# An attention and expert kernel: a chunk's right operands formed over two units, with raw weights in tiles of their own and the next pair's attention in every unit

## The chip, the cores and the metric

One Trainium2 chip, one core. A core has engines with their own instruction queues, each working through its queue in order: TensorE (PE; its weight loads stand as PEld), VectorE (DVE), ScalarE (ACT), GpSimd (POOL), and SyncE (SP), which here issues nearly all DMA transfers. The metric is the device time of one execution in microseconds (us).

## The reference, cut to what matters

```python
# q, k, v: (8, 8, 576, 64); p: (8, 8, 32, 64); w1: (4, 512, 1024); w2: (4, 1024, 512)
def sm_attn(qq, kk, vv):
    s = scale * np.matmul(qq, kk.transpose(0, 1, 3, 2))
    a = np.exp(s - np.max(s, axis=-1, keepdims=True))
    a = a / (np.sum(a, axis=-1, keepdims=True) + 1e-09)
    return np.matmul(a, vv)
p_packed = sm_attn(p, k, v)            # 32 packed tokens attend to all 576
x = sm_attn(q, p_packed, p_packed)     # all tokens attend to the packed ones
# x becomes (8*576, 512); pr = domain_probs, each row divided by its sum
for e in range(4):
    h = np.maximum(x @ w1[e], 0.0)
    out += pr[:, e:e + 1] * (h @ w2[e])
```

## The kernel before, in words

The work is split into 64 **units**. A unit is one batch (576 tokens) times one **chunk**, which is half an expert (512 of its 1024 hidden columns), so there are 8 chunks. Batches go in **pairs**: the units of the first pair are chunk 0 with batch 0, chunk 0 with batch 1, chunk 1 with batch 0, and so on (L283), 16 units for each of four pairs. In a pair of units the unit of the lower batch is called even, that of the upper batch odd.

A unit has two stages. `mm1_group` (L293) makes a block of the hidden layer, 24 matmuls of 128x288 each, four times a unit; VectorE multiplies it with the probabilities into a tile `ablk` (L311). `product` (L376) makes one of seven products of Strassen's kind, 12 matmuls each; their left operands are `ablk` blocks or sums of them (`sblk`, L328), and the right ones are blocks of w2 or differences of them. Every operand is kept as two parts, a rounded high part, cast by ScalarE (`hi_of`, L101), and the remainder, made by a subtraction (`lo_of`, L107). For the left operands the result is the tile `st` (four buffers), with the remainder on GpSimd; for the right ones it is `tt` (eight buffers). VectorE adds a product to its accumulator (`acc`, L394), or ScalarE copies it there when the chunk is the first (L392). The left operand of product i+2 is made while product i runs, and the hidden blocks of the next unit are made between the products of this one (`GROUPS`, L531).

`t_form` (L346) makes the seven right operands of a chunk: two raw halves of w2's chunk are loaded (L353), in-place differences t1 to t4 are taken (L366), and for each operand there is a cast on ScalarE and a subtraction on GpSimd (L369, L370). This is done in the first pair alone: each `tt` is stored to DRAM (`t_store`), and the three later pairs load it back (`t_load`). In the first pair it is done for chunk c+1 in the odd unit of chunk c, a step after each product (L573); its raw halves go into the tiles `kt` and `vt` of the pool `att`, which the attention uses too for k, q and v.

The attention of the next pair of batches also runs beside the units, as generators that are moved a step after certain products (`back`, L571): `pack_unit` (L140) for the packed tokens, and `tok_unit` (L213) for all tokens, each twice, for two halves of the heads. `AT_FIRST` (L533) says in which step (2 x chunk + 1 if odd) of the first pair each starts. `g_form` (L259) multiplies the packed tokens with the next chunk's w1 (tile `wraw`) into `ghl`, the weights of `mm1_group`.

PSUM has four double tiles `dbl`, which all matmuls share. The order of an engine's instructions isn't that of the code alone: the tile framework's scheduler puts the instructions of all generators into one order for each engine when the program is built.

The first 43 us or so are a prologue: attention of the first two batches, right operands of chunk 0 and the hidden blocks of unit 0.

## Time and profile before

| | us |
|---|---|
| median of three runs | 1331.51 (1331.44 to 1331.95) |
| the profiled execution | 1326.61 |
| its span, first to last instruction | 1324.8 |
| TensorE busy in the span | 1260.2 (95%) |
| VectorE busy | 950.8 (72%) |
| GpSimd busy | 862.5 (65%) |
| ScalarE busy | 474.8 (36%) |

The program is one long stretch of matmuls on TensorE with the other engines beside it, so it is read by pairs of units. A mark that recurs once in each pair of units is the group of 32 matmuls on `wraw` in `g_form`; from one such mark to the next is a *step pair* below. In the first pair of batches the marks start at 54.64, 105.72, 152.57, 198.74, 241.07, 284.15, 326.26 and 368.20 us, and the first one of the second pair of batches is at 407.91. Step pairs of the first pair of batches are counted from 0 (54.64 to 105.72) to 7 (368.20 to 407.91); those of the second pair, from 407.91 to 721.73, likewise.

### The profile page before, as it was taken

To read this page: it belongs to the slowest core of one execution; us is meant where nothing else is said; L and a number is where in the kernel's file an instruction comes from. 1 tells how busy PE (TensorE), PEld (TensorE's weight loads), DVE (VectorE), ACT (ScalarE), POOL (GpSimd) and SP (SyncE) were. 2 spreads that over 40 slices of the span, in tenths; PEclk is the share of its full clock that TensorE was granted. 3 is DMA by queue.
4 is the path that set the end of the run, shared out by engine and by line. 5 is a ranking of instruction groups with operands and counts; after the bars stand their busy time and mean duration, and the time that the engine had idled before them with its cause. 6 is when DMAs were issued, how large, how long until landed. Compare 5 with 4: busy or idle time off the path is not lost.

```text
span 1324.8 us, 26645 instructions
## 1 busy us (share of the span) xinstructions
PE 1260.2 (95%) x10720; PEld 1179.9 (89%) x10720; DVE 950.8 (72%) x1334; ACT 474.8 (36%) x784; POOL 862.5 (65%) x578
## 2 busy tenths in 40 slices
PE   4798998999999999999999999999999999999997
PEld 2697888889999989999999998999999999999996
DVE  5766779688685665888677566698668566666668
ACT  4353433434325423333333433333232533333231
POOL 5675787879887454467569554566657755555656
PEclk8999999999999999999999999999999999999999
DMA  9526643452465455544346554344454443344422
GB/s 359 199 82 214 205 162 114 177 186 105 187 208 165 157 175 175 188 148 136 119 133 215 175 171 151 127 150 150 124 153 175 159 134 123 123 152 137 127 96 72
DMA packets 84634, 208.98 MB, mean 158 GB/s; under 512 B 8608, under 2 KB 27168, under 8 KB 84512
## 3 DMA queue, kind: packets, MB, share of 16 engines
q1 hardware_dynamic: 83840, 207.13, 46.5%
q8 instruction: 86, 1.41, 0.4%
q14 instruction: 36, 0.29, 0.1%
q10 hardware_dynamic: 672, 0.15, 0.1%
HBM read 168.37 MB, written 38.87 MB: 156 GB/s over the span
## 4 chain that ended last, share of the span: by engine, by line
PE 74%; POOL 11%; DVE 6%; issue 5%; DMA 3%; ACT 1%; DVEq 0%; POOLq 0%; ACTq 0%; SPq 0%
PE dbl L66 70%; POOL st L108 5%; PE dbl L74 4%; POOL tt L108 3%; DMA kt<-in_w 2%; DVE sblk L328 1%; POOL kt L366 1%; DVE ghl L108 1%; DVE ablk L311 1%; POOL xl L108 1%; DVE acc L444 1%; DVE acc L409 1%; PE dbl L69 1%; POOL acc L444 1%; DMA pnd<-pb 1%
## 5 line engine op out<-in xcount | busy, mean ns | idle before, releaser
L66 PE MATMUL dbl<-st,tt 128*128 128x288 f32 x5376 | 771.7, 297 | 20.6 <-DVE ghl L108 8.3
L66 PEld LDWEIGHTS dbl<-st,tt 128*128 128x128 f32 x5376 | 731.3, 188 | 56.2 <-issue 27.6
L108 POOL TENSOR_TENSOR st<-sblk,st 128x576 fp32r<-128x576 f32 x256 | 394.4, 1548 | 250.9 <-ACT st L103 248.0
L66 PE MATMUL dbl<-xh,ghl 128*128 128x288 f32 x2048 | 416.7, 295 | 0.0
L108 POOL TENSOR_TENSOR st<-ablk,st 128x576 fp32r<-128x576 f32 x192 | 290.7, 1516 | 160.4 <-ACT st L103 159.8
L394 DVE TENSOR_TENSOR acc<-dbl,acc 128x576 f32<-128x576 f32 x385 | 288.6, 752 | 116.3 <-PE dbl L66 115.6
L66 PEld LDWEIGHTS dbl<-xh,ghl 128*128 128x128 f32 x2048 | 330.2, 189 | 0.0
L66 PE MATMUL dbl<-xl,ghl 128*128 128x288 f32 x1024 | 304.2, 297 | 18.1 <-DVE ablk L311 8.4
L311 DVE SCALAR_TENSOR_TENSOR ablk<-dbl,pbt 128x576 f32<-128x576 f32 x256 | 192.5, 752 | 166.0 <-PE dbl L66 164.5
L103 ACT CAST st<-sblk 128x576 fp32r<-128x576 f32 x256 | 173.1, 677 | 328.5 <-DVE sblk L328 230.1
L103 ACT CAST st<-ablk 128x576 fp32r<-128x576 f32 x192 | 129.6, 675 | 264.5 <-PE dbl L66 254.8
L66 PEld LDWEIGHTS dbl<-xl,ghl 128*128 128x128 f32 x1024 | 193.1, 189 | 20.7 <-DVE ablk L311 10.0
L328 DVE TENSOR_TENSOR sblk<-ablk 128x576 f32<-128x576 f32 x128 | 122.4, 956 | 9.2
L103 ACT CAST ghl<-dbl 128x512 fp32r<-128x512 f32 x128 | 71.9, 587 | 96.9 <-PE dbl L74 42.3
L108 DVE TENSOR_TENSOR ghl<-dbl,ghl 128x512 fp32r<-128x512 f32 x128 | 85.0, 684 | 24.5 <-ACT ghl L103 22.8
L328 DVE TENSOR_TENSOR sblk<-ablk,sblk 128x576 f32<-128x576 f32 x64 | 63.2, 988 | 3.1
L74 PE MATMUL dbl<-wraw,ppbd 64*32 64x512 f32 x1024 | 64.2, 595 | 0.3 <-ACT acc L392 0.3
L108 POOL TENSOR_TENSOR tt<-kt,tt 128x512 fp32r<-128x512 f32 x35 | 50.5, 1444 | 13.3 <-ACT tt L103 13.3
L328 DVE TENSOR_TENSOR sblk<-sblk,ablk 128x576 f32<-128x576 f32 x64 | 57.3, 895 | 1.4
L444 POOL TENSOR_TENSOR acc<-acc,acc 128x576 f32<-128x576 f32 x28 | 47.5, 1707 | 10.2 <-DVE acc L394 10.2
L392 ACT COPY acc<-dbl 128x576 f32<-128x576 f32 x56 | 35.6, 642 | 43.1 <-PE dbl L66 42.8
L103 ACT CAST tt<-kt 128x512 fp32r<-128x512 f32 x35 | 21.6, 621 | 46.1 <-DVE kt L366 16.7
(60 smaller groups left out, 442.4 us busy)
## 6 DMA issues: line engine op xcount, KB each, us to landing
tt<-td SPq DMA_DIRECT2D x168, 512.0 KB, 4.0
wraw<-in_w SPq DMA_DIRECT2D x128, 256.0 KB, 3.8
td<-tt SPq DMA_DIRECT2D x56, 512.0 KB, 4.4
kt<-in_k SPq DMA_DIRECT2D x16, 576.0 KB, 5.1
kt<-in_q SPq DMA_DIRECT2D x16, 576.0 KB, 5.3
pbt<-pnd SPq DMA_DIRECT2D x32, 288.0 KB, 4.0
out<-acc SPq DMA_DIRECT2D x32, 288.0 KB, 2.3
vt<-in_v SPq DMA_DIRECT2D x16, 512.0 KB, 5.8
```

The costliest lines, as they stand in the source:

```text
L66: on_pe(nc.tensor.matmul(**kw))
L69: on_pe(nc.tensor.transpose(**kw))
L74: ins = nc.tensor.matmul(**kw).ins
L103: nc.scalar.copy(out=dst, in_=src)
L108: eng.tensor_tensor(out=dst, in0=src, in1=hi.bitcast(F32), op=ALU.subtract)
L311: nc.vector.scalar_tensor_tensor(out=a, in0=ps[:, :, 0:HS], scalar=0.0, in1=pbt[b][:, ts].rearrange("p (o t) -> p o t", o=1).broadcast_to( ...
L328: nc.vector.tensor_tensor(out=t, in0=blk(x), in1=blk(y), op=op)
L366: eng[m].tensor_tensor(out=blk[place], in0=blk[x], in1=blk[y], op=ALU.subtract)
L392: nc.scalar.copy(out=accs[b, i], in_=psv)
L394: nc.vector.tensor_tensor(out=accs[b, i], in0=psv, in1=accs[b, i], op=ALU.add)
L409: nc.vector.tensor_tensor(out=dst, in0=x, in1=y, op=op)
L444: eng.tensor_tensor(out=m[dst], in0=m[x], in1=m[y], op=op)
```

## The change

Four edits, all in what the first pair of batches does.

1. Right operands of chunk c+1 are formed over both units of chunk c: three of them in the even one, after products 1, 3 and 5, and four in the odd one, after products 1 to 4 (`FORM`). `tt` has ten buffers in place of eight. A smaller scratch for dynamic DMA (`dynamic_dma_scratch_size=1024`) belongs to it; the kernel has no such DMA.
2. The raw halves of w2 have tiles of their own, `rw0` and `rw1`, one buffer each, and are loaded in the odd unit before, after products 3 and 5; those of chunk 1 before the first unit.
3. The subtraction t4 and the remainders of the operands `s3` and `a22` move from GpSimd to VectorE, beside t2 and t3, which were there. GpSimd keeps t1 and five remainders of seven.
4. The next pair's attention advances after every second product of every unit (before: in the even units alone, with all that was left drained at a unit's end for chunks 0 to 2), and its parts start at steps 3, 6, 9 and 12 in place of 2, 4, 6 and 10.

```diff
--- before.py
+++ after.py
@@ -336,38 +336,43 @@
     tt = {}
 
     def t_load(ch, i):
-        t = wpool.tile([P, 2, 2, DH], F32R, name="tt", bufs=8)
+        t = wpool.tile([P, 2, 2, DH], F32R, name="tt", bufs=10)
         nc.sync.dma_start(out=t.rearrange("p h f d -> p (h f d)").bitcast(F32), in_=td[ch][i])
         tt[ch, i] = t
 
     def t_store(ch, i):
         nc.sync.dma_start(out=td[ch][i], in_=tt[ch, i].rearrange("p h f d -> p (h f d)").bitcast(F32))
 
-    def t_form(ch, new, eng):
-
+    w2r = {}
+
+    def w2_load(ch, kh, new):
         e, hf = divmod(ch, F // FC)
-        raw = []
-        for kh in range(2):
-            r0 = hf * FC + kh * 2 * P
-            r = new([P, 2, DM], ("kt", "vt")[kh])
-            nc.sync.dma_start(out=r, in_=w2[e, r0:r0 + 2 * P, :].rearrange("(f p) d -> p f d", p=P))
-            raw.append(r)
+        r0 = hf * FC + kh * 2 * P
+        r = new([P, 2, DM], f"rw{kh}")
+        nc.sync.dma_start(out=r, in_=w2[e, r0:r0 + 2 * P, :].rearrange("(f p) d -> p f d", p=P))
+        w2r[ch, kh] = r
+
+    def raw_tile(shape, name):
+        return wpool.tile(shape, F32, name=name)
+
+    def t_form(ch, eng):
+
+        raw = [w2r.pop((ch, kh)) for kh in range(2)]
         blk = {
             "b11": raw[0][:, :, 0:DH], "b12": raw[0][:, :, DH:DM],
             "b21": raw[1][:, :, 0:DH], "b22": raw[1][:, :, DH:DM],
         }
-        yield
         of = {"a11": "b11", "a12": "b21", "s4": "b22", "a22": "t4", "s1": "t1", "s2": "t2", "s3": "t3"}
         how = {"t1": ("b12", "b11", "b11"), "t2": ("b22", "t1", "t1"), "t3": ("b22", "b12", "b12"), "t4": ("t2", "b21", "t2")}
         for i, name in enumerate(ORDER):
             n = of[name]
             for m in {"t3": ("t1", "t3"), "t2": ("t2",), "t4": ("t4",)}.get(n, ()):
                 x, y, place = how[m]
-                eng[m].tensor_tensor(out=blk[place], in0=blk[x], in1=blk[y], op=ALU.subtract)
+                eng.get(m, nc.gpsimd).tensor_tensor(out=blk[place], in0=blk[x], in1=blk[y], op=ALU.subtract)
                 blk[m] = blk[place]
-            t = wpool.tile([P, 2, 2, DH], F32R, name="tt", bufs=8)
+            t = wpool.tile([P, 2, 2, DH], F32R, name="tt", bufs=10)
             hi_of(t[:, 0], blk[n], nc.scalar)
-            lo_of(t[:, 1], blk[n], t[:, 0], nc.gpsimd)
+            lo_of(t[:, 1], blk[n], t[:, 0], eng.get(name, nc.gpsimd))
             tt[ch, i] = t
             yield
 
@@ -470,9 +475,6 @@
     def att_tile(b, shape, name):
         return att.tile(shape, F32, name=name, bufs=2 if name in ("kt", "a1") else 1)
 
-    def raw_tile(shape, name):
-        return att_tile(0, shape, name)
-
     hpool = ctx.enter_context(tc.tile_pool(name="hpool", bufs=1, reuse_waits="tile"))
     with ExitStack() as first:
         pools = [first.enter_context(tc.tile_pool(name=f"unit{u}", bufs=1)) for u in range(3)]
@@ -492,11 +494,12 @@
             tok_unit([b], g, unit_tile(2 * b + g), nc.gpsimd if g else nc.vector, nc.gpsimd if b else nc.scalar)
             for b in range(2) for g in range(NG)
         ]
-        forms = t_form(0, form_tile, {n: nc.gpsimd for n in ("t1", "t2", "t3", "t4")})
         norm_probs()
         for i in (0, 1, 0, 1):
             next(packs[i])
-        next(forms)
+        for kh in range(2):
+            w2_load(0, kh, form_tile)
+        forms = t_form(0, {})
         raws = w1_load(0)
         drain(wavefront(packs[:2], 1))
         for i in range(2):
@@ -530,7 +533,12 @@
     nothing = iter(())
     GROUPS = {1: ((0, 0),), 3: ((0, 1),), 4: ((1, 1),), 6: ((1, 0),)}
     GROUPS_FIRST = {4: ((0, 0), (0, 1)), 5: ((1, 1),), 6: ((1, 0),)}
-    AT_FIRST = ((2, pack_unit, 0), (4, pack_unit, 1), (6, tok_unit, 0), (10, tok_unit, 1))
+    AT_FIRST = ((3, pack_unit, 0), (6, pack_unit, 1), (9, tok_unit, 0), (12, tok_unit, 1))
+    FORM = ({1: 1, 3: 1, 5: 1}, {1: 1, 2: 1, 3: 1, 4: 1})
+    form_eng = {"t2": nc.vector, "t3": nc.vector, "t4": nc.vector, "s3": nc.vector, "a22": nc.vector}
+    for kh in range(2):
+        w2_load(1, kh, raw_tile)
+    tsteps = nothing
     AT_LATER = ((1, pack_unit, 0), (4, pack_unit, 1), (7, tok_unit, 0), (9, tok_unit, 1))
     sums, back = nothing, nothing
     for u, (sb, ch, b) in enumerate(units):
@@ -550,10 +558,8 @@
         if not odd and nsb < SB:
             gsteps = g_form([2 * nsb, 2 * nsb + 1], nch, raws)
         forming = odd and sb == 0 and ch + 1 < NCH
-        tsteps = nothing
-        if forming:
-            tsteps = t_form(ch + 1, raw_tile, {"t1": nc.gpsimd, "t2": nc.vector, "t3": nc.vector, "t4": nc.gpsimd})
-        next(tsteps, None)
+        if not odd and sb == 0 and ch + 1 < NCH:
+            tsteps = t_form(ch + 1, form_eng)
         for i in range(NPROD):
             product(u, i)
             n = i + LA
@@ -568,16 +574,17 @@
                 next(gsteps, None)
             if i == 4 and u + 2 < len(units) and units[u + 2][1] % 2 == 0:
                 load_probs(units[u + 2][2], units[u + 2][1] // 2)
-            if sb > 0 and i % 2 == 0 or sb == 0 and not odd and (i % 2 == 0 or ch < 3):
+            if i % 2 == 0:
                 next(back, None)
-            next(tsteps, None)
+            if i in FORM[odd]:
+                next(tsteps, None)
+            if forming and ch + 2 < NCH and i in (3, 5):
+                w2_load(ch + 2, i // 4, raw_tile)
             next(sums, None)
             if sb == 0 and not odd:
                 t_store(ch, i)
             if odd and nxt and not forming:
                 t_load(nxt[1], i)
-        if sb == 0 and ch < 3:
-            drain(back)
         drain(gsteps)
         drain(sums)
         if ch == NCH - 1 and b < B - 1:
@@ -610,7 +617,7 @@
         "w1": np.ascontiguousarray(moe_w1),
         "w2": np.ascontiguousarray(moe_w2),
     }
-    nc = bacc.Bacc("TRN2", target_bir_lowering=False, num_devices=1)
+    nc = bacc.Bacc("TRN2", target_bir_lowering=False, num_devices=1, dynamic_dma_scratch_size=1024)
     args = [
         nc.dram_tensor(f"in_{n}", arrays[n].shape, mybir.dt.from_np(arrays[n].dtype), kind="ExternalInput").ap()
         for n in _INS
```

What this does to the order on the engines, at three places. On ScalarE, around the casts of `ghl` in an even unit. Before (`kt` is the raw half of w2, `st` a left operand):

```order
L103 CAST st<-ablk 128x576 [waits PE_49,Pool_49]
L171 ACTIVATE a_1813,sm<-dbl,nb 128x576 [waits DVE_49,PE_49]
L103 CAST st<-ablk 128x576 [waits PE_49,Pool_49]
L171 ACTIVATE a_1822,sm<-dbl,nb 128x576 [waits DVE_49]
L103 CAST tt<-kt 128x512 [waits DMAHW3_49,DMAHW0_49]
L103 CAST ghl<-dbl 128x512 [waits PE_49]
L103 CAST ghl<-dbl 128x512 [waits DVE_49]
L103 CAST ghl<-dbl 128x512 [waits PE_49]
```

And now (`rw_1514` is a raw half of chunk 3, `at` an attention tile):

```order
L103 CAST tt<-rw_1514 128x512 [waits DMAHW2_49,DVE_49]
L103 CAST tt<-rw_1514 128x512 [waits DMAHW4_49,Pool_49]
L188 COPY at<-dbl 128x512 [waits PE_49]
L189 COPY at<-dbl 64x128
L103 CAST st<-ablk 128x576 [waits PE_49,Activation_49]
L103 CAST st<-sblk 128x576 [waits DVE_49,PE_49,Activation_49]
L103 CAST st<-ablk 128x576 [waits PE_49,Pool_49]
L103 CAST st<-ablk 128x576 [waits DVE_49,PE_49,Pool_49]
L103 CAST ghl<-dbl 128x512 [waits PE_49]
L103 CAST ghl<-dbl 128x512 [waits DVE_49]
L103 CAST ghl<-dbl 128x512 [waits PE_49]
L103 CAST st<-sblk 128x576 [waits PE_49,Pool_49]
```

Before, the first cast of a chunk, which waits for the raw half to land, stood right ahead of the casts of `ghl`; now the first three casts of a chunk stand ahead of a run of left operands, and the `ghl` casts have no raw half ahead of them in their unit.

On GpSimd, in an odd unit. Before (`kt` and `vt` raw halves, L366 the subtraction t4):

```order
L108 TENSOR_TENSOR tt<-kt,tt 128x512 [waits DMAHW5_49,Activation_49]
L108 TENSOR_TENSOR tt<-kt,tt 128x512 [waits DMAHW2_49,Activation_49]
L108 TENSOR_TENSOR st<-sblk,st 128x576 [waits Activation_49]
L108 TENSOR_TENSOR st<-ablk,st 128x576 [waits Activation_49]
L108 TENSOR_TENSOR tt<-kt,tt 128x512 [waits DMAHW3_49,Activation_49]
L108 TENSOR_TENSOR st<-ablk,st 128x576 [waits Activation_49]
L366 TENSOR_TENSOR kt<-kt,vt 128x2x256 [waits DMAHW6_49,Pool_49]
L108 TENSOR_TENSOR st<-sblk,st 128x576 [waits Activation_49]
L108 TENSOR_TENSOR tt<-kt,tt 128x512 [waits Activation_49]
L108 TENSOR_TENSOR tt<-vt,tt 128x512 [waits Activation_49]
L108 TENSOR_TENSOR tt<-vt,tt 128x512 [waits DMAHW7_49,Activation_49]
L108 TENSOR_TENSOR st<-sblk,st 128x576 [waits Activation_49] x2
```

And now, from the remainder of `s2` (the fourth operand) of chunk 4 to that of the third operand of chunk 5 (`rw_2075` and `rw_2129` are chunk 4's raw halves, `rw_2604` is chunk 5's, L371 is t1):

```order
L108 TENSOR_TENSOR tt<-rw_2075,tt 128x512 [waits DMAHW4_49,Activation_49]
L108 TENSOR_TENSOR st<-ablk,st 128x576 [waits Activation_49]
L108 TENSOR_TENSOR st<-sblk,st 128x576 [waits Activation_49]
L108 TENSOR_TENSOR tt<-rw_2129,tt 128x512 [waits DMAHW5_49,DMAHW0_49,Activation_49]
L108 TENSOR_TENSOR st<-ablk,st 128x576 [waits Activation_49]
L108 TENSOR_TENSOR tt<-rw_2129,tt 128x512 [waits DMAHW1_49,Activation_49]
L108 TENSOR_TENSOR st<-ablk,st 128x576 [waits Activation_49]
L108 TENSOR_TENSOR tt<-rw_2604,tt 128x512 [waits DMAHW7_49,DMAHW3_49,Activation_49]
L108 TENSOR_TENSOR st<-sblk,st 128x576 [waits Activation_49]
L371 TENSOR_TENSOR rw_2604<-rw_2604 128x2x256 [waits Pool_49]
L108 TENSOR_TENSOR st<-sblk,st 128x576 [waits Activation_49] x2
L108 TENSOR_TENSOR tt<-rw_2604,tt 128x512 [waits DMAHW6_49,Activation_49]
```

Before, seven instructions of the forming stand among these thirteen; now five remainders and t1 stand among seven left operands, and after the last row seven left operands follow with no forming between them. The first remainder of a chunk, which needs its raw half, stands four left operands behind the remainder of `s2`, ahead of where the code has it.

On VectorE, where t3 stands (it takes the second raw half, and waits for GpSimd's t1). Now, at the end of an odd unit (`acc` accumulators, `ablk` a hidden block out of PSUM):

```order
L311 SCALAR_TENSOR_TENSOR ablk<-dbl,pbt 128x576 [waits PE_49]
L328 TENSOR_TENSOR sblk<-ablk 128x576 [waits DVE_49]
L399 TENSOR_TENSOR acc_1101<-dbl,acc_1101 128x576 [waits PE_49]
L328 TENSOR_TENSOR sblk<-sblk,ablk 128x576 [waits DVE_49,Pool_49]
L399 TENSOR_TENSOR acc_1121<-dbl,acc_1121 128x576 [waits PE_49]
L371 TENSOR_TENSOR rw_2075<-rw_2129,rw_2075 128x2x256 [waits DMAHW5_49,DMAHW2_49,Pool_49]
L311 SCALAR_TENSOR_TENSOR ablk<-dbl,pbt 128x576 [waits PE_49]
L328 TENSOR_TENSOR sblk<-ablk,sblk 128x576 [waits DVE_49,Activation_49]
L108 TENSOR_TENSOR tt<-rw_2075,tt 128x512 [waits DMAHW1_49,Activation_49]
```

Before, in the even unit that holds the mark of step pair 4:

```order
L108 TENSOR_TENSOR ghl<-dbl,ghl 128x512 [waits Activation_49] x3
L394 TENSOR_TENSOR acc_796<-dbl,acc_796 128x576 [waits PE_49]
L366 TENSOR_TENSOR kt<-vt,kt 128x2x256 [waits DMAHW6_49,DMAHW7_49,DMAHW4_49,Pool_49]
L311 SCALAR_TENSOR_TENSOR ablk<-dbl,pbt 128x576 [waits PE_49]
L328 TENSOR_TENSOR sblk<-ablk 128x576 [waits DVE_49]
L394 TENSOR_TENSOR acc_845<-dbl,acc_845 128x576 [waits PE_49]
```

At both places a block that leaves PSUM stands right behind t3; what moved is t3 against the units, from behind the `ghl` remainders to behind the odd unit's last accumulation, and a remainder (the last row of the first piece) is new on this engine.

## Rows read from the trace of the kernel before

**Rows 1.** The page, part 1: busy us, share of the span and instructions of each engine.

```profile
PE 1260.2 (95%) x10720; PEld 1179.9 (89%) x10720; DVE 950.8 (72%) x1334; ACT 474.8 (36%) x784; POOL 862.5 (65%) x578
```

**Rows 2.** Windows: length, busy us (instructions) of each engine, granted clock, DMA share, GB/s.

```profile
54.64:105.72 51.08, 44.62 (x352) 41.46 (x352) 31.43 (x39) 23.02 (x41) 42.26 (x31) 0.93 0.34 119
105.72:368.20 262.48, 240.18 (x2058) 223.84 (x2057) 202.85 (x275) 100.54 (x172) 209.75 (x142) 0.99 0.48 169
...
407.91:448.08 40.17, 40.17 (x376) 37.44 (x375) 22.10 (x35) 19.00 (x34) 24.23 (x18) 1.00 0.53 176
448.08:683.02 234.94, 232.81 (x2011) 219.35 (x2010) 173.69 (x258) 79.04 (x126) 132.67 (x89) 1.00 0.47 153
...
241.07:284.15 43.08, 40.32 (x329) 37.72 (x329) 30.76 (x42) 14.72 (x24) 39.12 (x28) 0.96 0.58 210
...
569.28:608.21 38.93, 38.75 (x329) 36.18 (x329) 34.92 (x53) 14.22 (x22) 25.30 (x17) 1.00 0.48 160
```

**Rows 3.** Waits of TensorE from 105.72 to 368.20: total us, times, longest.

```profile
PE dbl L66 <- DVE ghl L108: 10.4, 4, 3.5
PE dbl L66 <- DVE ablk L311: 6.6, 4, 2.9
PE dbl L66 <- POOL st L108: 3.0, 4, 1.2
```

**Rows 4.** Timeline of TensorE: start, us, instruction, idle before and releaser.

```profile
112.11 0.38 PE L66 MATMUL dbl<-xl,ghl 128*128 128x288 f32 x1 [2.16 <-DVE ghl L108]
...
207.58 3.43 PE L66 MATMUL dbl<-st,tt 128*128 128x288 f32 x24 [3.50 <-DVE ghl L108]
...
252.38 0.40 PE L66 MATMUL dbl<-xl,ghl 128*128 128x288 f32 x1 [2.76 <-DVE ablk L311]
```

**Rows 5.** Two pieces of the chain that ended last: start, us, matmuls.

```profile
252.38 27.32 PE dbl L66 x192
...
647.78 35.33 PE dbl L66 x264
```

**Rows 6.** Timeline of the other engines around the forming.

```profile
108.79 0.62 ACT L103 CAST tt<-kt 128x512 fp32r<-128x512 f32 x1 [2.60 <-DMA kt<-in_w]
...
126.50 0.69 DVE L366 TENSOR_TENSOR kt<-vt,kt 128x512 f32<-128x512 f32 x1 [1.34 <-DMA vt<-in_w]
...
250.68 0.97 DVE L366 TENSOR_TENSOR kt<-vt,kt 128x512 f32<-128x512 f32 x1 [4.29 <-POOL kt L366]
...
258.08 1.29 POOL L108 TENSOR_TENSOR tt<-kt,tt 128x512 fp32r<-128x512 f32 x1 [0.98 <-ACT tt L103]
```

**Rows 7.** Timeline: GpSimd and VectorE instructions that overlap.

```profile
225.82 3.34 POOL L108 TENSOR_TENSOR st<-ablk,st 128x576 fp32r<-128x576 f32 x2
...
227.84 1.93 DVE L328 TENSOR_TENSOR sblk<-ablk 128x576 f32<-128x576 f32 x1
...
229.12 1.81 POOL L108 TENSOR_TENSOR tt<-kt,tt 128x512 fp32r<-128x512 f32 x1
```

**Rows 8.** VectorE by line: two groups from 105.72 to 368.20, one from 448.08 to 683.02.

```profile
L328 DVE TENSOR_TENSOR sblk<-ablk 128x576 f32<-128x576 f32 x24 | 27.4, 1140 | 1.0
...
L366 DVE TENSOR_TENSOR kt<-vt,kt 128x512 f32<-128x512 f32 x12 | 15.0, 1247 | 14.4 <-POOL kt L366 6.5 <-POOL st L108 4.8 <-DMA vt<-in_w 2.0
...
L328 DVE TENSOR_TENSOR sblk<-ablk 128x576 f32<-128x576 f32 x24 | 19.2, 798 | 1.7
```

**Rows 9.** DMA issues from 100 to 400 us: count, KB, us to landing.

```profile
kt<-in_w SPq DMA_DIRECT2D x6, 512.0 KB, 5.9
vt<-in_w SPq DMA_DIRECT2D x6, 512.0 KB, 7.5
```

**Rows 10.** Timeline, the prologue and step pair 0.

```profile
29.95 0.74 ACT L171 ACTIVATE a<-dbl,nb 128x576 f32<-128x576 f32 x1 [2.21 <-DVE nb L168]
...
58.52 1.25 POOL L366 TENSOR_TENSOR kt<-kt 128x512 f32<-128x512 f32 x1
...
63.36 0.61 PE L66 MATMUL dbl<-xl,ghl 128*128 128x288 f32 x1 [4.99 <-POOL xl L108]
```

## The prediction

> **What bounds the kernel now.** First the page: TensorE is busy for 1260.2 of 1324.8 us [rows 1], so it is the bound, and nothing can be won but in what it idles or does slowly. The next view says where that is. The windows between the marks of the step pairs show the first pair of batches beside the second, which does the same matmuls without the forming [rows 2]: step pairs 1 to 6 take 262.48 us in the first and 234.94 in the second, 27.54 longer, and step pair 0 takes 51.08 against 40.17. Of the 27.54 a part is work: 2058 matmuls against 2011. At 240.18 / 2058 = 0.117 each the 47 are at most 5.5, so 22 to 27.5 us are lost in this stretch, and it is the stretch where the forming stands.
>
> Then the waits of TensorE in that stretch [rows 3]: 10.4 for `ghl`, 6.6 for `ablk`, 3.0 for `st`, 20.0 together. The timeline says what is behind each [rows 4]. The wait at 112.11 is for `ghl`, whose cast stood on ScalarE behind a cast of `tt` that waited 2.60 for the raw half `kt` to land [rows 6]; 207.58 is of the other kind, `ghl` late on VectorE beside a token step of the attention. The wait at 252.38 is for `ablk`: VectorE had stood 4.29 at t3, waiting for GpSimd's t1 [rows 6], with the hidden block queued behind it. After that wait the matmuls are slow for a while: 192 of them take 27.32, where 264 elsewhere take 35.33, or 0.134 each, so 25.7 for 192 [rows 5]. That is 1.6 lost, and the granted clock of this step pair is 0.96 [rows 2], which is 8% of 43.08, or 3.4 us, at 1.2 in place of 2.4 GHz, worth 1.7.
>
> **The change part by part.** All sums are against the profiled execution's 1326.61, of which 1.8 lies outside the span; the median of the runs shown is 4.90 above it, and I carry that over.
>
> *Raw weights in their own tiles.* The load no longer waits for the attention's `kt`, and the first cast of a chunk no longer stands ahead of `ghl`. Of the four `ghl` waits, two are of this kind, together 3.6 (the shown 2.16 and its like): I take all of it off. The other two, together 6.8 (the shown 3.50 and its like), lie at the token steps, where VectorE is crowded. The token step is now stepped in odd units too, but VectorE gets more to do beside it. Bounds 0 and 6.8; I take half, 3.4, as the row has neither edge on its side.
>
> *Forming over two units.* GpSimd's t1 came late because the odd unit holds thirteen instructions with seven of the forming among them; now the forming is spread, t1 stands behind the next chunk's first remainder and well ahead of where VectorE gets to t3, which follows the odd unit's last accumulation. Of the 6.6 for `ablk`, two waits (2.76 shown, 2.9 the longest) make 5.7, and each has its slow stretch of 1.65: 5.7 + 3.3 = 9.0 off. The rest, 0.9, stays. Of the 3.0 for `st`, which are GpSimd being full, the longest is 1.2, and there are two such: 2.3 off.
>
> *Three instructions from GpSimd to VectorE.* t4 and two remainders per chunk, 18 in six step pairs. On VectorE such a subtraction takes from 0.69 [rows 6] to a mean of 1.25 [rows 8], so 12.4 to 22.5 more. VectorE's 202.85 [rows 2] becomes at most 225.4 of about 246, 92%. The second pair of batches has a step pair with 34.92 of 38.93, 90%, in which TensorE was busy for 38.75 of 38.93 [rows 2]. So the average fits, with nothing to spare. Covered by TensorE: cost zero on average, and the crowding is what I left in the token term.
>
> *New waits.* The raw half `rw0` is reloaded behind the remainder of `a22` and must be there for the next chunk's first cast, which the order on GpSimd puts four left operands and two remainders behind `s2`'s remainder. Counted from there: t4, cast, remainder (0.69 to 1.25, 0.62, 0.69 to 1.25), then 5.9 to 7.5 to land [rows 6, 8, 9], 7.9 to 10.6 us. GpSimd needs 4 x 1.67 + 2 x 1.29 = 9.3 meanwhile [rows 6, 7]. So it arrives between 1.4 before its need and 1.3 after. ScalarE stands there with left operands queued behind, and TensorE notices only when the two made ahead are used up, 2 x 12 to 24 matmuls x 0.134 = 3.2 to 6.4 us. Bounds per step pair 0 and 2.6 (the wait that was there before [rows 6]), in six 0 to 15.6. I take 0.25 each, 1.5, near the lower end, since the arrival is.
>
> *Prologue and step pair 0.* Chunk 1's raw halves are loaded before unit 0, 1 MB ahead of the stores, and its first three operands are formed there. ScalarE waits 2.21 at 29.95 anyway [rows 10], which hides the first cast; but on VectorE t3, a remainder and t2 now stand ahead of the first `ablk`: 3 x 0.69 to 1.25, 2.1 to 3.75 later. In return t1 (1.25 at 58.52) and a remainder (1.29) are gone from the chain on GpSimd that TensorE waits 4.99 for at 63.36 [rows 6, 10]: 2.5 earlier. Net between -2.5 and +3.75; the two nearly cancel, I take 0.
>
> *Two more `tt` buffers, and the later pairs.* TensorE has no wait for a reloaded `tt` among those above; their stretch 448.08 to 683.02 is busy for 232.81 of 234.94 [rows 2], so a gain or a loss there is within 2: zero.
>
> Sum: -3.6 - 3.4 - 9.0 - 2.3 + 1.5 = -16.8. 1326.61 - 16.8 = 1309.8, and with the 4.90 **1314.7 us**.
>
> **The rivals.** *GpSimd and VectorE as one resource.* At 227.84 a sum on VectorE takes 1.93, and ends with GpSimd's operand at 229.16 and 0.6 more; GpSimd's next instruction, from 229.12, takes 1.81 where 1.29 is usual [rows 6, 7]. The first kind of `sblk` has a mean of 1140 ns with the forming and of 798 without [rows 8]. So the two seem to take turns, and what moves from one to the other still holds both. Then the edit is worth the difference alone, 1.29 - 0.69 = 0.6, 18 times: 10.8, if that pair is what TensorE waits for. For it: GpSimd is busy for 39.12 of 43.08 in step pair 4. Against it: 209.75 of 262.48, 80%, over all six, so spreading must help beyond that. The time: 1326.61 - 10.8 + 4.9 = 1320.7. The Trainium skill has this as a rule (SBUF — State Buffer, Who interferes with whom): a VectorE instruction with two SBUF inputs contends with a GpSimd instruction that reads SBUF, and whoever comes first holds the port for its whole instruction. By that rule, the trace agrees, with 1.93 at 227.84.
>
> *All of it comes back.* Step pairs 1 to 6 run like those of the second pair of batches: 27.54 less about 1.2 for the attention step more, 26.3 off, 1305.2. For it: the deadlines of the operands become a whole unit looser. Against it: the second pair has no forming, and leaves VectorE at 173.69 of 234.94 [rows 2].
>
> *Slower: t3 as a gate in every step pair.* VectorE takes its queue in order, and t3 now needs two raw halves, the second loaded only after the odd unit's last remainder, and t1. If it is late, the hidden block behind it stays in PSUM and TensorE stops, as at 252.38: 2.85 and 1.65 of slow clock, 4.5 each time. Six times make 27.0 in place of the 18.3 removed: 8.7 slower, 1340.2. It decides from 18.3 / 6 = 3.05 us per step pair on. Against it: t1 stands early in GpSimd's order now.
>
> *No change.* TensorE's losses stay, only their releasers change: the forming's sum of work is the same, and 20 us of waits [rows 3] find other names. 1331.5.
>
> **How the numbers follow.** Forecast 0.57, one resource 0.15, all back 0.16, no change 0.05, slower 0.07. The forecast's own range is 1308 to 1321, from the token term (3.4 either way) and the prologue (-2.5 to +3.75). The range of 8 in 10 takes in the first two rivals and some of the new waits: 1303 to 1328. Within 0.2% (2.7 us) a measurement of this kernel can't be told from no change. Faster 0.57 + 0.15 + 0.16 = 0.88, same 0.05, slower 0.07.
>
> **What would show it.** Right: step pairs 1 to 6 at about 246 us; no cast of `tt` waiting for a raw half just ahead of `ghl`; no idle VectorE of 4 us at t3; the granted clock at 1.00 there; waits that stay lie at the token steps. Wrong: TensorE waiting for `st` or `ablk` at the end of odd units, with VectorE at t3 or ScalarE at the first cast of a chunk behind it; a first hidden block more than 4 us later than before; or VectorE busy over 95% in the stretch.

## The result, and the profile after

The changed kernel takes 1319.78 us, the median of six runs (1319.35 to 1322.56), against 1331.76 for the kernel before in the same comparison: a ratio of 0.9906, 95% interval [0.9891, 0.9921], or 12.5 us less (10.5 to 14.5); the two medians alone differ by 12.0. That is faster, inside the range of 1303 to 1328, and 5.1 us above the forecast of 1314.7.

The two profiled executions lie closer together, 1321.78 against 1326.61, 4.8 us. The first experiment shows why: the profile on record of the kernel before was a short execution.

The page first, the line that answers to [rows 1]: VectorE has 27 us more, GpSimd 21 less.

```profile
PE 1266.0 (96%) x10720; PEld 1184.1 (90%) x10720; DVE 977.7 (74%) x1355; ACT 476.0 (36%) x784; POOL 841.5 (64%) x557
```

The windows by marks, as in [rows 2]: step pairs 1 to 6 of the first pair of batches, then of the second.

```profile
108.30:364.15 255.85, 242.35 (x2090) 224.20 (x2089) 226.52 (x298) 101.63 (x172) 189.58 (x123) 0.99 0.48 168
442.96:677.92 234.96, 232.81 (x2011) 219.35 (x2011) 173.72 (x258) 79.06 (x126) 132.74 (x89) 1.00 0.46 153
```

The first was to be about 246 and is 255.85, in place of 262.48, with 2090 matmuls in it in place of 2058. The second is as it was.

TensorE's waits in that stretch, the counterpart of [rows 3] (total us, times, longest):

```profile
PE dbl L66 <- DVE nb L168: 3.2, 2, 1.7
PE dbl L69 <- DVE ppn L200: 2.8, 1, 2.8
PE dbl L66 <- DVE acc L399: 2.3, 2, 1.9
PE dbl L66 <- POOL st L108: 2.2, 3, 1.3
PE dbl L66 <- DVE ablk L311: 1.4, 1, 1.4
```

The 10.4 for `ghl` are gone, and 6.6 for `ablk` have become 1.4. New are `nb` and `acc`, and `ppn` has 2.8 in place of 0.8; `nb` and `ppn` are small steps inside the attention's own chain. The timeline of the longest, cut to the rows that matter, shows what is ahead of it (GpSimd, VectorE, then TensorE; it answers to [rows 4, 7]):

```profile
223.09 3.25 POOL L108 TENSOR_TENSOR st<-sblk,st 128x576 fp32r<-128x576 f32 x2
223.23 1.82 DVE L371 TENSOR_TENSOR rw<-rw,rw 128x512 f32<-128x512 f32 x1
226.30 1.71 POOL L108 TENSOR_TENSOR tt<-rw,tt 128x512 fp32r<-128x512 f32 x1
226.81 1.81 DVE L328 TENSOR_TENSOR sblk<-ablk,sblk 128x576 f32<-128x576 f32 x1
228.55 0.27 DVE L200 TENSOR_SCALAR ppn<-dbl,rs 128x64 f32<-128x64 f32 x1
228.87 0.30 PE L69 MATMUL dbl<-ident,ppn 128*64 128x128 f32 x1 [2.80 <-DVE ppn L200]
```

The `ppn` that TensorE waits for takes 0.27, but stands behind a sum that takes 1.81 beside a running GpSimd instruction. VectorE's queue is now where the time goes.

Marks move in TensorE's order with the change, so from here on I count by units: unit u begins with the first of its 84 matmuls of products. These starts are worked out from the trace (us, and what the stretch takes):

```
                      before      e1     after
unit 0 begins          47.72    47.89     52.07
unit 2 begins          94.02    94.18     97.08
units 2 to 5           92.31    94.41     82.56
units 6 to 15         211.19   215.83    212.76
unit 16 to the end    927.28   927.48    927.30
```

The prologue costs 3 and the later pairs nothing. Units 2 to 5, where the attention of the next pair used to be pressed into two even units, are 9.75 shorter, but a part of that is work that has moved. Windows of units 2 to 5 and 6 to 15, of before and of after:

```profile
94.02:186.33 92.31, 84.77 (x842) 77.43 (x841) 66.58 (x99) 36.41 (x68) 66.31 (x47) 1.00 0.55 185
186.33:397.52 211.19, 194.67 (x1546) 182.65 (x1545) 170.91 (x219) 76.86 (x127) 177.47 (x118) 0.98 0.48 169
```

```profile
97.08:179.64 82.56, 79.52 (x718) 74.44 (x717) 69.83 (x92) 33.51 (x58) 62.65 (x42) 1.00 0.51 184
179.64:392.40 212.76, 200.51 (x1670) 185.44 (x1669) 191.80 (x244) 79.27 (x133) 160.04 (x102) 0.98 0.47 164
```

124 matmuls have moved from the first stretch to the second, so 5.3 of the 9.75 is moved work. Together the two stretches are busy for 280.03 (279.44 before), and idle for 15.29 in place of 24.06; of these 8.8 us, 4.5 are in units 2 to 5 and 4.3 in units 6 to 15.

### The profile page after: what moved, and what is told of

The parts are those of the page before. It is cut to its first block, busy times and chain, and to the rows that moved or that the text cites. A ratio compares the mean times of both kernels' runs of the same rounds, so it can differ in the third digit from the quotient of the medians.

```text
span 1319.7 us, 26624 instructions
## 1 busy us (share of the span) xinstructions
PE 1266.0 (96%) x10720; PEld 1184.1 (90%) x10720; DVE 977.7 (74%) x1355; ACT 476.0 (36%) x784; POOL 841.5 (64%) x557
## 4 chain that ended last, share of the span: by engine, by line
PE 79%; DVE 11%; POOL 4%; issue 2%; DMA 2%; ACT 1%; DVEq 0%; SPq 0%; ACTq 0%; POOLq 0%
PE dbl L66 74%; PE dbl L74 5%; DVE sblk L328 2%; POOL st L108 2%; DVE ablk L311 1%; DVE acc L399 1%; DVE rw L371 1%; DVE ghl L108 1%; DMA rw<-in_w 1%; DVE tt L108 1%; PE dbl L69 1%; DVE acc L414 1%; POOL tt L108 1%; DVE acc L449 1%; DMA pnd<-pb 1%
## 5 line engine op out<-in xcount | busy, mean ns | idle before, releaser
L108 POOL TENSOR_TENSOR st<-sblk,st 128x576 fp32r<-128x576 f32 x256 | 399.1, 1566 | 262.1 <-ACT st L103 259.2
L108 DVE TENSOR_TENSOR ghl<-dbl,ghl 128x512 fp32r<-128x512 f32 x128 | 85.0, 684 | 20.9 <-ACT ghl L103 19.3
L108 POOL TENSOR_TENSOR tt<-rw,tt 128x512 fp32r<-128x512 f32 x35 | 51.4, 1468 | 14.9 <-ACT tt L103 14.7
L103 ACT CAST tt<-rw 128x512 fp32r<-128x512 f32 x49 | 29.4, 620 | 47.7 <-DVE rw L371 24.1
```

The source lines that it names most:

```text
L103: nc.scalar.copy(out=dst, in_=src)
L108: eng.tensor_tensor(out=dst, in0=src, in1=hi.bitcast(F32), op=ALU.subtract)
```

## The experiments

All ratios are to the kernel before. A difference of two ratios is given with the root of the sum of their squared half widths, and in us it is that difference times 1331.76; it can be some 2 us from the difference of the two medians. "Idle" is TensorE's, in units 2 to 15, from windows like those above; a part of a difference in time is the clock, which stands in the busy time. The timelines are cut to the rows that matter.

| run | what it is | us | ratio [95%] | idle |
|---|---|---|---|---|
| e1 | before again | 1332.74 | 0.9992 [0.9979, 1.0005] | 25.7 |
| e5 | tiles alone | 1328.17 | 0.9958 [0.9944, 0.9972] | 23.1 |
| e6 | tiles, attention | 1327.45 | 0.9951 [0.9934, 0.9968] | 19.7 |
| e4 | all but the attention | 1328.22 | 0.9961 [0.9948, 0.9974] | 20.8 |
| e3 | all but the three on VectorE | 1324.68 | 0.9937 [0.9913, 0.9961] | 20.9 |
| e2 | all but the forming's spread | 1323.74 | 0.9925 [0.9901, 0.9949] | 17.7 |
| after | all | 1319.78 | 0.9906 [0.9891, 0.9921] | 15.3 |
| e7 | and chunk 0 through `rw` | 1320.84 | 0.9910 [0.9890, 0.9931] | 15.2 |
| e8 | and t1, s1 on VectorE | 1328.73 | 0.9963 [0.9949, 0.9976] | 19.5 |
| e10 | t2, t3, s3 on VectorE | 1324.96 | 0.9935 [0.9915, 0.9956] | 20.9 |
| e9 | t3, s3 on VectorE | 1317.96 | 0.9898 [0.9871, 0.9925] | 15.5 |
| e11 | t3, s3, t4, a22 on VectorE | 1316.92 | 0.9880 [0.9866, 0.9893] | 15.3 |
| e12 | e9, attention as before | 1329.54 | 0.9970 [0.9959, 0.9980] | 23.3 |

**e1, the kernel before again.** No edit.

> The kernel before, unchanged, to see how far one profiled execution stands for all. The profiled execution on record took 1326.61 us, the timed ones 1331.5. If that 4.9 us is a fixed cost of a timed execution, a second profile lasts 1326.6 again with step pairs 1 to 6 at 262.5. If the executions differ by their clock or their first loads, a second profile lasts 1330 to 1333, and the difference lies ahead of unit 2.

The second profile lasts 1333.64, so 4.9 is no fixed cost; where the difference lies I had wrong. It is in units 2 to 10, in waits a little longer and in the clock after them. The same piece, units 6 and 7, in the profile on record and in this one:

```profile
186.33:231.31 44.98, 39.54 (x331) 36.27 (x329) 40.23 (x55) 16.21 (x27) 35.01 (x24) 1.00 0.44 156
```

```profile
188.59:236.18 47.59, 41.94 (x330) 38.91 (x329) 40.43 (x55) 16.24 (x27) 34.34 (x24) 0.93 0.43 147
```

The same work has 2.4 us more of busy TensorE at a mean granted clock of 0.93. Against this second profile the changed kernel's is 11.9 shorter, which agrees with the medians.

**e2, the forming in one unit.** Seven operands in the odd unit, the raw halves reloaded at its end.

```diff
-    FORM = ({1: 1, 3: 1, 5: 1}, {1: 1, 2: 1, 3: 1, 4: 1})
+    FORM = ({}, {i: 1 for i in range(NPROD)})
...
+        if forming and ch + 2 < NCH:
+            for kh in range(2):
+                w2_load(ch + 2, kh, raw_tile)
```

> The changed kernel with all seven operands formed in the odd unit, as before (raw halves reloaded at its end). Theory of the forecast (deadlines of the forming): the waits for ablk and st and their slow stretches come back, 9.0 + 2.3 = 11.3 us, so about 1331. One resource (GpSimd and VectorE take turns): the sum of the forming's work is the same and only its place differs, 0 to 3 us, 1320 to 1323.

1323.74: undoing the spread costs 0.0019 ± 0.0028, 2.5 us and not told from nothing, in place of 11.3, and inside the 0 to 3 of *one resource*. The forecast's largest term falls.

**e3, t4 and two remainders back on GpSimd.**

```diff
-    form_eng = {"t2": nc.vector, "t3": nc.vector, "t4": nc.vector, "s3": nc.vector, "a22": nc.vector}
+    form_eng = {"t2": nc.vector, "t3": nc.vector}
```

> The changed kernel with t4 and the remainders of s3 and a22 back on GpSimd. One resource: what holds the pair grows by 18 x 0.6 = 10.8 us, so about 1330.6. Theory of the forecast: the share between the engines costs nothing on average; GpSimd goes from 189.6 to 215 of 256 us in step pairs 1 to 6 and waits for st come back, at most the 3.0 they were, 1320 to 1323.

1324.68, 4.1 us more (0.0031 ± 0.0028): more than the forecast's zero, less than half of the other's. The timeline shows a third cause (GpSimd, VectorE, TensorE):

```profile
109.07 1.29 POOL L108 TENSOR_TENSOR tt<-rw,tt 128x512 fp32r<-128x512 f32 x1
110.39 1.87 DVE L371 TENSOR_TENSOR rw<-rw,rw 128x512 f32<-128x512 f32 x1 [2.57 <-POOL tt L108]
112.18 0.68 DVE L108 TENSOR_TENSOR ghl<-dbl,ghl 128x512 fp32r<-128x512 f32 x1
114.35 2.98 PE L66 MATMUL dbl<-st,tt 128*128 128x288 f32 x11 [3.85 <-DVE ghl L108]
```

t2 overwrites t1's block and must wait for the remainder of `s1`, which GpSimd has behind that of `s3`. VectorE stands for 2.57 with `ghl` queued behind, and TensorE for 3.85. The idle time of VectorE ahead of the forming's subtractions over the first pair (from 94 to 400 us; last the idle time) is 9.6 here and 5.1 in the changed kernel:

```profile
L371 DVE TENSOR_TENSOR rw<-rw,rw 128x512 f32<-128x512 f32 x12 | 20.7, 1721 | 9.6 <-POOL rw L371 5.3 <-POOL tt L108 4.3
```

```profile
L371 DVE TENSOR_TENSOR rw<-rw,rw 128x512 f32<-128x512 f32 x18 | 28.8, 1602 | 5.1 <-POOL rw L371 3.6 <-POOL tt L108 0.9 <-issue 0.6
```

**e4, the attention at its old places.**

```diff
-    AT_FIRST = ((3, pack_unit, 0), (6, pack_unit, 1), (9, tok_unit, 0), (12, tok_unit, 1))
+    AT_FIRST = ((2, pack_unit, 0), (4, pack_unit, 1), (6, tok_unit, 0), (10, tok_unit, 1))
...
-            if i % 2 == 0:
+            if sb > 0 and i % 2 == 0 or sb == 0 and not odd and (i % 2 == 0 or ch < 3):
...
+        if sb == 0 and ch < 3:
+            drain(back)
```

> The changed kernel with the next pair's attention at its old places (steps 2, 4, 6, 10, even units only, finished at a unit's end in the first three chunks). Theory of the forecast: the waits for ghl at the token steps come back, 3.4 of 6.8 us, so about 1323. Rival (the spread attention costs what it saves): the new waits of the changed kernel for the attention's own chain (nb, ppn and s, 6.7 us) go, and 6.8 for ghl come, so 1320 within 2. Rival (the attention in every unit only adds waits): the 6.7 go and nothing comes back, 1313.

1328.22, 7.3 us more (0.0055 ± 0.0020), beyond each of the three. TensorE's waits in units 2 to 15 here:

```profile
PE dbl L66 <- DVE ablk L311: 6.1, 5, 1.4
PE dbl L66 <- POOL st L108: 4.5, 6, 1.3
PE dbl L66 <- DVE ghl L108: 3.8, 2, 1.9
```

The forming is spread, and yet `ablk` has 6.1, and `st` 4.5, more than the 3.4 to 4.0 of before in the same units. The two long waits for `ablk`, those of units 9 and 13 before, are gone, but four of 1.4 stand in units 2, 4, 6 and 10. So the spread doesn't bring the time without the attention's new places. e2 and e6 are the other half of this: forming in one unit, attention spread, and 4.6 and 2.6 for `ablk`.

**e5, the raw tiles alone.** The edits of e2, e3 and e4 together, and, in both places that make a `tt`:

```diff
-            t = wpool.tile([P, 2, 2, DH], F32R, name="tt", bufs=10)
+            t = wpool.tile([P, 2, 2, DH], F32R, name="tt", bufs=8)
```

> The kernel before with the raw halves in tiles of their own and loaded a chunk ahead, and nothing else of the change (forming in the odd unit, t4 and the remainders on GpSimd, attention at its old places, eight buffers). Forecast's own term: two waits for ghl go, 3.6 us, and their like in slow clock, so 1327 to 1329. If the earlier forming of chunk 1 delays the first unit by 2.5 us, as the traces of the other runs show, 1330 to 1332. If the tiles are what the attention's places need and worth nothing alone: 1331.5 to 1334.

1328.17, 5.6 us less than before (0.0042 ± 0.0014), the forecast's own figure with the clock. `ghl`, 10.9 of wait in units 2 to 15 before (12.2 in e1), has 3.2; but others are there now, and the idle time is 23.1, where it was 24.1 before and 25.7 in e1:

```profile
PE dbl L66 <- DVE ablk L311: 6.8, 5, 1.9
PE dbl L66 <- DVE acc L399: 6.2, 4, 2.4
PE dbl L66 <- DVE rs L176: 3.6, 2, 1.8
PE dbl L66 <- DVE ghl L108: 3.2, 4, 1.0
```

e4, which has the spread, the ten buffers and the three instructions on VectorE besides, isn't faster than this (0.0003 ± 0.0019).

**e6, the tiles and the attention's new places.** The edits of e2 and e3 together:

```diff
-    FORM = ({1: 1, 3: 1, 5: 1}, {1: 1, 2: 1, 3: 1, 4: 1})
+    FORM = ({}, {i: 1 for i in range(NPROD)})
...
+    form_eng = {"t2": nc.vector, "t3": nc.vector}
```

> The changed kernel with the forming in the odd unit and t4 and two remainders on GpSimd: tiles of their own, ten buffers and the attention's new places remain. If the attention's places are the main cause (units 2 to 5 are 12 us shorter with them), about 1324 to 1327, and units 2 to 5 take 83 to 85 us. If the parts need each other (the spread attention only fits where the forming has left GpSimd free), 1329 to 1332.

1327.45, a little above the first range: on the tiles alone (and with ten `tt` buffers in place of eight) the attention's places are worth 0.0007 ± 0.0022, not told from nothing. Units 2 to 5 take 87.38 and not 83 to 85, since the stall at t2 of e3 is there too:

```profile
112.83 6.10 PE L66 MATMUL dbl<-st,tt 128*128 128x288 f32 x24 [2.96 <-DVE ghl L108]
```

The wait is 2.96, and the 24 matmuls behind it take 6.10, at a mean granted clock of 0.51, where 24 at full clock take 3.43 [rows 4]: 5.6 us in all.

**e7, chunk 0 through the raw tiles.**

```diff
-            w2_load(0, kh, form_tile)
+            w2_load(0, kh, raw_tile)
```

> The changed kernel with chunk 0's raw halves in the tiles that chunk 1's then wait for. If two instructions for chunk 1 ahead of the attention's on GpSimd are what begins unit 0 2.3 to 4.4 us later than before, unit 0 begins 2.5 us earlier, and the time is 1317.3. If the later start comes from the loads or from the clock granted there, nothing moves: 1319.8. If chunk 1's operands then come late, unit 2 waits for them, up to 3 us the other way, 1322.

1320.84, no change, and unit 0 begins at 52.34. GpSimd did have the attention's instructions first, so what I read in its order is not what delays the first unit.

**e8, two more kinds on VectorE.**

```diff
-"s3": nc.vector, "a22": nc.vector}
+"s3": nc.vector, "a22": nc.vector, "t1": nc.vector, "s1": nc.vector}
```

> The changed kernel with t1 and the remainder of s1 on VectorE as well. One resource: what holds the pair falls by 14 x 0.6 = 8.4 us, half of it where TensorE waits, so 1311 to 1316. If VectorE's own queue is the limit now (88% busy in step pairs 1 to 6, 99% with 14 to 26 us more), 1322 to 1335, with waits for ppn, nb and acc.

1328.73, 7.6 us slower than the changed kernel (0.0057 ± 0.0020), where one resource has it faster. VectorE hardly waits for GpSimd any more (0.9 of the 1.3 idle ahead of the same subtractions), and a subtraction takes 1095 ns in place of 1602:

```profile
L371 DVE TENSOR_TENSOR rw<-rw,rw 128x512 f32<-128x512 f32 x18 | 19.7, 1095 | 1.3 <-POOL tt L108 0.9 <-DMA rw<-in_w 0.4
```

But TensorE now has 6.0 of wait for `nb` in units 2 to 15, in place of 3.2, and 5.8 for `acc`, in place of 4.4; `ppn`, with 3.0, is about as it was. The longest of them, with t1 on VectorE ahead of it (VectorE, TensorE):

```profile
132.47 1.92 DVE L371 TENSOR_TENSOR rw<-rw 128x512 f32<-128x512 f32 x1
138.98 0.61 PE L66 MATMUL dbl<-xl,ghl 128*128 128x288 f32 x1 [4.14 <-DVE nb L168]
```

VectorE works without a gap from that t1 to the end of `nb`. The same wait is 1.72 in the changed kernel: VectorE's queue is the limit.

**e9 and e10, which of the forming stands on VectorE.** e9 has t3 and the remainder of `s3` there; e10 has t2 as well, and differs in nothing else.

```diff
-    form_eng = {"t2": nc.vector, "t3": nc.vector, "t4": nc.vector, "s3": nc.vector, "a22": nc.vector}
+    form_eng = {"t3": nc.vector, "s3": nc.vector}
```

> The changed kernel with t3 and the remainder of s3 alone on VectorE; t2, t4 and the remainder of a22 on GpSimd. Against e3 one instruction of a kind is exchanged for another (s3's remainder for t2), so each engine has as many of the forming's as there. Hand-off (VectorE stands at t2 until GpSimd has done s1's remainder, with ghl queued behind, 3.85 us and 2.1 of slow clock at 114.35 in e3): no such hand-off is left, VectorE idles 4 to 6 us less ahead of the forming's subtractions than the 9.6 of e3, and the time is 1318 to 1321. One resource, or GpSimd's load: as e3, 1324.7.

> The changed kernel with t4 and the remainder of a22 back on GpSimd; the remainder of s3 stays on VectorE. Hand-off: s3's remainder stood ahead of s1's on GpSimd, for which t2 waits, so it carries most of what the three are worth (4.1 us between e3 and the changed kernel): 1320 to 1321.5. One resource: a third of it, 7 x 0.6 x the same share, 1323.3.

e9 does as the hand-off has it: 1317.96, not told from the changed kernel (0.0008 ± 0.0031), and 4.2 of idle VectorE ahead of the subtractions, 5.4 less than in e3. The median of e10 misses both expectations (by its ratio, 1323.1 ± 2.7 on the base of 1331.76, the 1323.3 of one resource isn't ruled out): its idle VectorE is low too, 3.7, and it takes 1324.96, 4.9 us more than e9 (0.0037 ± 0.0034). So VectorE waiting is not the whole of it. The same place in both, first e10:

```profile
107.90 1.98 POOL L108 TENSOR_TENSOR st<-ablk,st 128x576 fp32r<-128x576 f32 x1
108.50 1.93 DVE L371 TENSOR_TENSOR rw<-rw,rw 128x512 f32<-128x512 f32 x1
110.35 0.68 DVE L108 TENSOR_TENSOR ghl<-dbl,ghl 128x512 fp32r<-128x512 f32 x1
112.52 4.94 PE L66 MATMUL dbl<-st,tt 128*128 128x288 f32 x24 [2.17 <-DVE ghl L108]
```

and e9:

```profile
108.06 0.68 DVE L108 TENSOR_TENSOR ghl<-dbl,ghl 128x512 fp32r<-128x512 f32 x1
109.40 1.27 POOL L371 TENSOR_TENSOR rw<-rw,rw 128x512 f32<-128x512 f32 x1
110.23 1.97 PE L66 MATMUL dbl<-st,tt 128*128 128x288 f32 x13 [0.28 <-DVE ghl L108]
```

In e10 t2 stands ahead of `ghl` and takes 1.93, beside a GpSimd instruction that ends at 109.88; TensorE waits 2.17, and 24 matmuls behind that take 4.94, at a mean granted clock of 0.65. In e9 GpSimd does t2 in 1.27, in time that it had over, and TensorE waits 0.28. This unit makes 3.4 of the 7.3 us by which units 2 to 15 of e10's profile are longer; units 6 and 10 make 1.8 and 1.6. Here a subtraction on VectorE costs what is queued behind it. The changed kernel has t2 on VectorE too, but there it stands at 105.38, ahead of the group on `wraw` at 108.30, and TensorE has no wait for `ghl`: an exchange makes the order of the queues anew.

**e11, t2 alone moved to GpSimd.**

```diff
-    form_eng = {"t2": nc.vector, "t3": nc.vector, "t4": nc.vector, "s3": nc.vector, "a22": nc.vector}
+    form_eng = {"t3": nc.vector, "s3": nc.vector, "t4": nc.vector, "a22": nc.vector}
```

> The changed kernel with t2 alone on GpSimd in place of VectorE. Between e10 and e9 that one exchange is worth 7 us (1324.96 against 1317.96). If t2 on VectorE costs as much in the changed kernel too, because it stands there with the hidden block and ghl queued behind, about 1313 to 1315. If it cost that only where s1's remainder was late on GpSimd, which in the changed kernel it is not (0.9 us of idle VectorE there against 4.3 in e3), 1319 to 1321. One resource: 7 x 0.6 more, 1322 to 1324.

1316.92, between the first two, and 3.5 us less than the changed kernel (0.0026 ± 0.0020): the fastest version here, though not told from e9. That t2's place is the reason isn't shown: TensorE idles for 15.3 us of units 2 to 15 in both. By the profiles 3.0 of the 5.0 us between the two spans lie ahead of unit 2, and the other 2.0 are busy time, that is, clock.

**e12, e9 with the attention at its old places.** The edit of e9 and that of e4.

> The kernel of e9 with the next pair's attention at its old places. If the attention's place is worth its 8 us wherever no hand-off takes the gain (it was 1 us between e5 and e6, with a stall of 3.25 and 2.45 of slow clock at t2 in e6, and 8 between e4 and the changed kernel), 1324 to 1327, with units 2 to 5 at 91 to 95 us in place of 83.5. If what matters is how full VectorE is, and the forming's lighter share in e9 leaves room for the crowded units, 1318 to 1321.

1329.54, a little above the first range: 9.6 us more than e9 (0.0072 ± 0.0029), with VectorE's share of the forming as light as there. Units 2 to 5 of e9 and of e12:

```profile
94.93:178.47 83.54, 81.12 (x718) 75.98 (x717) 62.39 (x86) 33.68 (x60) 68.42 (x48) 0.98 0.50 178
```

```profile
94.98:185.09 90.11, 84.64 (x842) 77.42 (x841) 67.13 (x100) 36.19 (x67) 68.85 (x48) 1.00 0.56 192
```

TensorE idles 5.5 of the second and 2.4 of the first, at 74% and 75% of busy VectorE. The place of the attention counts, not VectorE's average.

## Why the prediction was right, and where it was wrong

The sign and the range were right; the sum of -16.8 was 4.3 too large, and its terms were less good than the sum: the largest was far too large, three others too small, and that this nearly cancelled is luck. Of what was to show it, the `ghl` waits behind a cast and the 4 us of idle VectorE at t3 are gone (2.6 is the longest left, at 98.61). But of the 15.3 us of waits that stay in units 2 to 15 only 6.7 are the attention's (`nb`, `ppn` and `s`), the granted clock is 0.99, and step pairs 1 to 6 are 10 above the 246, some 3.7 of it for 32 matmuls more.

- **The base.** Carrying the 4.90 over was right only because the change was also judged by medians. It was no fixed cost but an execution with less slow clock than others: its mean granted clock is 0.990, where the 56 timed runs of the same kernel beside the experiments have 0.980 to 0.987, and 1330.64 us or more.
- **Raw tiles, -3.6.** Right in sign, -5.6 measured (e5), and the mechanism holds in part: the `ghl` waits lost 7.7 in units 2 to 15, but `acc` and `rs`, which had none, took 9.8. Against e1's profile idle time fell by 2.6; of the rest, 2.8 is busy time, that is, clock, and 1.1 lies ahead of unit 2.
- **Forming over two units, -9.0 and -2.3.** This is the step that failed. "Of the 6.6 for `ablk`, two waits (2.76 shown, 2.9 the longest) make 5.7, and each has its slow stretch": both were read rightly. The one at 252.38 has VectorE idle for 4.29 ahead of t3, and its like 4.76 (VectorE, TensorE, in the kernel before):

```profile
336.34 0.69 DVE L366 TENSOR_TENSOR kt<-vt,kt 128x512 f32<-128x512 f32 x1 [4.76 <-POOL st L108]
337.75 0.40 PE L66 MATMUL dbl<-xl,ghl 128*128 128x288 f32 x1 [2.95 <-DVE ablk L311]
```

  What failed is that the cure was credited to the spread alone. e2 measures 2.5 us for it, not told from zero. The two waits are gone with the spread (e4), but also without it, where the attention is at its new places (e6, e2), and the raw tiles alone bring them down to 1.89 and 1.85 (e5). And others come in their place: in units 2 to 15 `ablk` had 7.5 of wait before, and with the attention at its old places it keeps 6.8 (e5), 6.1 (e4, forming spread) and 3.2 (e12); with the new ones it has 1.9 (after), 2.6 (e6), 4.6 (e2, forming in one unit as in e6) and 4.7 (e9). So the waits under this one name don't follow the attention (from e12 to e9 they grow); what falls each time is the idle time as a whole.
- **The token steps, -3.4.** This was the attention's term, taken as half of 6.8 beside a row with neither edge. Its size was wrong: 7.3 (e4) to 9.6 (e12) beside the other parts, and nothing on the tiles alone (e6). A part of what I missed is in units 2 to 5, where the old rule pressed the two pack steps into units 2 and 4, and the prediction spoke of the token steps alone: 3.8 of the 5.5 us of idle time between e4 and the changed kernel, and 3.1 of the 7.8 between e12 and e9.
- **t4 and two remainders, 0.** Measured -4.1 (e3), and not by VectorE's average, from which I argued. The order of the queue sets it, as far as the places shown go: t2 stood waiting for GpSimd (e3), or ahead of `ghl` (e10). That t2, which the change leaves on VectorE, costs anything where it stands in the changed kernel isn't shown (e9, e11).
- **New waits, +1.5.** ScalarE does wait for a raw half at a chunk's first cast, three times and 8.6 us in units 2 to 15; the longest:

```profile
303.65 0.62 ACT L103 CAST tt<-rw 128x512 fp32r<-128x512 f32 x1 [3.06 <-DMA rw<-in_w]
```

  The next wait of TensorE ends at 316.10 and is for `acc`, and behind the other two none ends within 6 us. From that I put the price at 0; it was not tried apart.
- **Prologue, 0 within -2.5 and 3.75.** Unit 2 begins 2.9 to 3.1 later. e7 refutes the cause that I had for it. Ahead of unit 0, which begins 4.35 later, TensorE is busy for 32.96 in place of 29.59, at a granted clock of 0.80 in place of 0.89, and idle for 19.1 in place of 18.1; so most of it stands in slow matmuls, and why the clock is lower there stays open.
- **Later pairs, 0.** 927.30 against 927.28 and 927.48: right.

Of the rivals, *one resource* came nearest by its number, 1320.7, and fell by its mechanism: two more kinds on VectorE made it slower (e8). The turns that it rests on are real. [rows 7] and e10 agree with the Trainium skill (SBUF — State Buffer, Who interferes with whom) that the one that comes first keeps the port; but that sets what an instruction costs, 1.93 in place of 0.69 [rows 6], and not whether TensorE waits for it. *All of it comes back* fell, with 15.3 of idle time left; its 26.3 also takes for waiting what the prediction's first paragraph has as work, up to 5.5 of the 27.54. *No change* has a true part: e5 loses most of the `ghl` waits and keeps 23.1 us of idle time, under other names. *t3 as a gate* did not come: 5.1 of idle VectorE ahead of the forming's subtractions, in place of 14.4 [rows 8].

What stays open is how the parts act together. On the tiles alone the attention's places are worth nothing (e6 against e5), and so is all the rest without them (e4 against e5); both together are worth 6.9 us (the changed kernel against e5, 0.0052 ± 0.0021). Taken out of the changed kernel one at a time, the spread, the three instructions and the attention's places cost 2.5, 4.1 and 7.3, which is twice that: they aren't terms to be added, as the prediction added them. The stall at t2 may account for 5.6 us of what the attention's places lack in e6; the remainder was not isolated.

## What to carry to other kernels

Before crediting a wait to the edit that is aimed at it, list everything that is queued on the late engine in the same units, and ask which of it the change also moves. Parts that are taken out one at a time needn't add up; add them one at a time as well. A price by average load says little for an engine that works in order: look at which instruction stands right ahead of the one that TensorE needs, whether it waits for another engine, and whether it can be done elsewhere. And take the base of a sum from more than one execution if the profiled one is off the median.

## What was not expected of the hardware

The same wait can be followed by half clock or not. In the changed kernel and in e7, which are alike there, TensorE waits 2.80 for `ppn`; the stretch behind it ran at full clock in the first, and at a mean of 0.64, in part at 1.2 GHz in place of 2.4, in the second:

```profile
228.90:232.20 3.30, 3.30 (x25) 3.30 (x26) 2.38 (x5) 0.68 (x1) 1.56 (x2) 1.00 0.43 171
```

```profile
228.86:233.60 4.74, 4.74 (x25) 4.74 (x26) 2.38 (x5) 0.68 (x1) 2.17 (x2) 0.64 0.30 119
```

The same 25 matmul records take 4.74 in place of 3.30. In the kernel before, the wait of 3.50 at 207.58 [rows 4] had no such stretch, and its like in e1 (3.94, at 210.30) was followed by a mean of 0.55. So a wait's price is itself plus, in some executions, 1.4 us or more, and one profile shows only one draw of it. The Trainium skill (TensorE: Matmul & The Clock Gate, The HAM clock gate) says that how many matmuls run at the low clock at a kernel's start varies between runs of one kernel; here, in the middle of one, even whether any do varied, for one and the same wait.
